# A table of times in a planned three-stage kernel: weight conversions, weight loads and operand splits at other places

## The chip, the cores and the metric

The kernel runs as one program on one core of a Trainium2 chip. The metric is device time in microseconds (us) of one execution; before the change it is the median of three runs, and one more execution was profiled. Engines are named as in the profile: PE is TensorE (its weight loads, which overlap its matmuls, are PEld), DVE is VectorE, ACT is ScalarE, POOL is GpSimd, SP is SyncE, which here only issues DMAs.

## The reference

Three things are computed in a row, in float32. First an attention in chunks of 64 positions, over batch 8, 8 heads, 576 positions and head size 64. Then a layer with softmax and layer norm, 512 to 1024 to 512. Then a layer with a SiLU, 512 to 2048 to 512:

```python
x = attention(q, k, v)                       # chunks of 64, softmax, 4608 tokens x 512
h = x @ w_in                                 # 512 -> 1024
solu = h * softmax(h)
ln = (solu - mean) / sqrt(var + 1e-06) * g_ln
x = ln @ w_out                               # 1024 -> 512
h = x @ w2_in                                # 512 -> 2048   ("the way in")
out = (h * sigmoid(h)) @ w2_out              # 2048 -> 512   ("the way out")
```

The weights come as 64-bit floats and are taken apart word by word on the chip.

## The kernel before

**Precision.** Each float32 operand of a matmul is split in two parts, hi (rounded on the way) and lo (the rest), and a product is three matmuls: hi by hi, hi by lo, lo by hi. A "split" is thus one copy to hi (ACT) and one subtraction for lo (DVE or POOL).

**Stages.** From 0 to about 598 us the attention and the first layer run for 36 tiles of 128 tokens. From 598.5 to 985.3 us the way in runs. From 985.3 us to the end the way out runs. Both ways use a scheme of seven products in place of eight (Strassen's), named p1, p6, p2, p7, p5, p4, p3 in the order in which PE makes them.

**The way in** takes the tokens in six groups of 768. A group needs seven split operands (`s_split`, tile `y1s`), made from four raw quarters of the input (`raw_load`, tile `ry`) and their differences (`raw_t`, POOL, L517). In a group there are eight units u, one for each slice of the weights, handled in four pairs. In a pair, PE makes each of the seven products for both units, 6 matmuls a product. Results are put together in this order: `c_p1` (ACT, L592), `c_u2` (DVE, L596), `c_u3` (DVE, L600), `c22` (DVE L610, then ACT), `c21` (L618), `c12` (L626). Each takes one buffer of a ring (`tmp`) and its result is stored to DRAM (`g_store`, tile `gd`, L588). PE may not start p7 before `c_u2` has read the bank that p6 left, and may not start p3 before `c22` has read the bank (`hw`) that p5 left: three products later in both cases.

**Changes of group.** While the last pair of a group runs, the operands of the next group are split, one after another as the product that used the old one ends. I count them 1 to 5; they lie at about 653, 713, 777, 838 and 903 us.

**The way out's weights** are converted during the way in, 16 pieces i = 0 to 15 (`conv_load`, `conv_a` L159, L160, `conv_b` L174, L185, `conv_c` L207, mostly on DVE), each from a 512 KB load into the tile `st_w`. Every two pieces are then mixed and split on POOL (`w2_mix`, L237, L248, L252) and stored to DRAM (`w2od`, L255). The attention tiles before carry the conversions of the way in's weights in the same functions.

**The way out** takes 18 pairs of token tiles. All its weights (56 tiles of 256 KB, `w2o_load`, tile `w2o`, L644) are read back from DRAM while the last group of the way in gives up its buffers. For each pair, four loads of 512 KB (`g_load`, L674), sums (`g_sum`, L681), splits (`g_split`, ACT L688, then DVE or POOL L690), seven products of 24 matmuls (`out_product`, L697), and stores (L723).

**What sets the order.** Every piece of work is entered in a plan with a time (`at(time, function, ...)`), and each engine, SP with its DMAs included, gets its instructions in the order of these times. The times are only sort keys: an engine runs its list in order and waits where data are missing. `XA` is the planned start of the way in, `PA` = 14 * 1.042 the planned length of a pair, so a group is 4 PA and a change of group falls on 4, 8, 12, 16 and 20 PA; `XB = XA + 24 * PA` is the planned start of the way out.

Of the kernel before, what the change touches and what calls it, by code (L numbers as in the profile page):

```python
# [18 lines left out]
DVE, POOL, ACT = ET.DVE, ET.Pool, ET.Activation  # L19
# [32 lines left out]
def chunk_attention_moe_moe(ctx: ExitStack, tc: tile.TileContext, q, k, v, w_in, w_out, g_ln, w2_in, w2_out, out):  # L52
# [44 lines left out]
    kT = sb.tile([128, 2 * HP, 2, CH], F32, tag="kT", name="kT")  # L97
# [629 lines left out]
    at = plan.at  # L727
# [24 lines left out]
    for t in range(TT):  # L752
# [32 lines left out]
            at(x + y[2], y_store, b, m)  # L785
        x = T[t]
        for _ in range(CONV[t] if nxt < N1 else 0):
            at(x - 10.0, conv_load, nxt)
            at((x + 2.0, x + 2.6), conv_a, nxt)
            at((x + 3.5, x + 4.1), conv_b, nxt, side(nxt))  # L790
            if nxt < 4 * KD:
                at((x + 5.2, x + 6.0, x + 6.7, x + 8.8), conv_c, nxt, side(nxt))
            else:
                at(x + 5.2, conv_c, nxt, side(nxt))
                if nxt % 2:
                    y = 122.2 if nxt == 17 else x + 5.3
                    at([y, y + 0.9, y + 1.8, y + 2.7] + [y + 3.6 + 3.8 * (i // 3) + (0.0, 1.0, 2.6)[i % 3] for i in range(12)], w2_mix, (nxt - 17) // 2, 0)
            nxt += 1
# [36 lines left out]
    for n in range(NGR * NF // 2):  # L835
# [13 lines left out]
            at([y + 12 * SL + d for d in (0.0, 0.6, 1.2)], c12, u)  # L849
        if jj == 0:  # L850
            x -= PA
            on = ((ACT, DVE), (ACT, DVE), (ACT, POOL), (ACT, DVE), (ACT, POOL), (ACT, POOL), (ACT, DVE))
            for o, (hi_on, lo_on) in enumerate(on):
                y = x + (2 * o + 2) * SL + 0.2
                if p == 0:
                    y = XO + 1.0 + 2.0 * o if o < 5 else XA + 0.3 + 1.2 * o - 6.0
                at((y, y + 1.0), s_split, p, o, hi_on, lo_on)
                if o in (0, 2):
                    at(y + 1.1, raw_t, p, 2 if o == 0 else 3)
            if p + 1 < NGR:  # L860
                y = x + PA * (2.05 if p == 0 else 1.5)
                for i, q4 in enumerate((1, 0, 2, 3)):
                    at(y + 0.7 * i, raw_load, p + 1, q4)
                at(x + PA * (3.75 - 1.2 * (p % 2)), raw_t, p + 1, 0)
                at(x + PA * (3.9 - 1.2 * (p % 2)), raw_t, p + 1, 1)

    for i in range(K2):
        n = N1 + i
        x = XA + PA * (8 * (i // 6) + (0.9, 1.55, 2.6, 3.2, 5.4, 6.1)[i % 6])
        at(x - (5.0 if i else 11.0), conv_load, n)  # L870
        at((x, x + 1.2), conv_a, n)
        at((x + 2.4, x + 3.6), conv_b, n)
        at(x + 4.8, conv_c, n)
        if i % 2:
            x += (0.35, 1.2, 0.35)[i % 6 // 2] * PA
            at([x + 0.8 * d for d in range(4)] + [x + 3.2 + 1.8 * (d // 3) + (0.0, 0.7, 1.5)[d % 3] for d in range(21)], w2_mix, i // 2, 1)
    XB = XA + 24 * PA
    SB = 24 * 0.12
    for when, step, tags in (
        (XB - 2.98 * PA, 1.15, ("wo", "wo", "wo")),  # L880
        (XB - 1.98 * PA, 1.1, ("wo", "u", "u", "wi", "wi", "wi", "wi")),
        (XB - 11.0, 1.05, ("wi", "wi", "wi", "wi", "xs", "vt", "vt")),
        (XB + 3.8, 0.75, ("qr", "qr", "kr", "kr", "kT", "pT", "qT", "e")),
    ):
        for tag in tags:
            n = UNITS.get(tag, 2)
            at([when + step * 2 * k for k in range(n // 2 + 1)], w2o_load, tag, BUFS.get(tag, 2), n)
            when += step * n
# [7 lines left out]
    for vp in range(NP):  # L896
        x = XB + 7 * SB * vp
        for i in (2, 3, 0, 1):
            y = XB - (3.6 - 0.2 * i) * PA if vp == 0 else XB + 0.3 if vp == 1 and i > 1 else max(x - 11 * SB, XB + 2.1)
            at(y + 0.1 * i, g_load, vp, i)  # L900
        for n in range(4):
            y = x + (-6.2, -5.7, -3.2, -0.9)[n] * SB
# [178 lines left out]
```

## Time and profile before

| | |
|---|---|
| median of 3 runs | 1369.13 us (1368.89 to 1372.35) |
| the profiled execution | 1366.64 us, of which the span from first to last instruction is 1364.8 us |
| mean granted PE clock | 0.983 |
| PE busy | 1280.3 us, 94% of the span |
| DVE, ACT, POOL busy | 900.1, 608.7, 587.4 us |

A row of the timeline gives start, length, engine, source line and operation, with the idle time before it and what ended that wait in brackets. A row of the windows gives busy time of each engine in a stretch, the granted PE clock (1.00 is 2.4 GHz, 0.50 is 1.2 GHz), the busy share of the DMA engines and the rate in GB/s.

### The profile page before, as it was taken

To read this page: it belongs to the slowest core of one execution; us is meant where nothing else is said; L and a number is where in the kernel's file an instruction comes from. 1 tells how busy PE (TensorE), PEld (TensorE's weight loads), DVE (VectorE), ACT (ScalarE), POOL (GpSimd) and SP (SyncE) were. 2 spreads that over 40 slices of the span, in tenths; PEclk is the share of its full clock that TensorE was granted. 3 is DMA by queue.
4 is the path that set the end of the run, shared out by engine and by line. 5 is a ranking of instruction groups with operands and counts; after the bars stand their busy time and mean duration, and the time that the engine had idled before them with its cause. 6 is when DMAs were issued, how large, how long until landed. Compare 5 with 4: busy or idle time off the path is not lost. (4 is left out here: it accounts for less than half of the span.)

```text
span 1364.8 us, 22483 instructions
## 1 busy us (share of the span) xinstructions
PE 1280.3 (94%) x8400; PEld 1169.4 (86%) x8400; DVE 900.1 (66%) x1371; ACT 608.7 (45%) x991; POOL 587.4 (43%) x466
## 2 busy tenths in 40 slices
PE   3889998999999999899899999989879999999998
PEld 2678886877887788788899999989879999999998
DVE  7798785877878788425555655563556666666661
ACT  5686544544554555433444434443333333443341
POOL 4543112321321332223554546262166666666662
PEclk9999998999999999999999999999889999999999
DMA  9575366655554651867576556659974434434420
GB/s 204 86 136 97 62 119 154 135 126 123 136 129 112 154 147 46 321 236 247 160 233 212 179 182 199 202 163 286 318 291 133 147 109 135 146 122 136 133 90 30
DMA packets 330845, 217.50 MB, mean 159 GB/s; under 512 B 187248, under 2 KB 288624, under 8 KB 330736
## 3 DMA queue, kind: packets, MB, share of 16 engines
q1 hardware_dynamic: 330736, 216.07, 56.2%
q8 instruction: 66, 1.08, 0.3%
q14 instruction: 43, 0.35, 0.1%
HBM read 130.03 MB, written 85.98 MB: 158 GB/s over the span
## 5 line engine op out<-in xcount | busy, mean ns | idle before, releaser
L580 PE MATMUL h<-y1s,w2t 128*128 128x384 f32 x1440 | 263.8, 338 | 9.6 <-DVE tmp L596 8.5
L697 PE MATMUL h<-w2o,gs 128*128 128x256 f32 x2160 | 265.7, 283 | 0.6 <-DMA w2o<-w2od 0.6
L580 PEld LDWEIGHTS h<-y1s,w2t 128*128 128x128 f32 x1440 | 252.9, 189 | 13.4 <-DVE tmp L596 11.5
L697 PEld LDWEIGHTS h<-w2o,gs 128*128 128x128 f32 x2160 | 262.2, 192 | 1.2 <-DMA w2o<-w2od 1.0
L407 PE MATMUL h<-wi,xs 128*128 128x512 f32 x864 | 220.2, 405 | 5.7 <-DVE u L424 2.9
L466 PE MATMUL yp<-lnT,wo 128*128 128x512 f32 x864 | 211.9, 395 | 0.7 <-ACT ys L471 0.7
L407 PEld LDWEIGHTS h<-wi,xs 128*128 128x128 f32 x864 | 162.1, 192 | 44.7 <-ACT e L346 2.9
L466 PEld LDWEIGHTS yp<-lnT,wo 128*128 128x128 f32 x864 | 159.1, 188 | 38.6 <-issue 5.1
L688 ACT ACTIVATE gs<-g 128x1024 fp32r<-128x1024 f32 x117 | 123.4, 1058 | 149.8 <-PE h L697 73.8
L690 POOL TENSOR_TENSOR gs<-g,gs 128x1024 fp32r<-128x1024 f32 x54 | 148.1, 2744 | 58.3 <-ACT gs L688 51.2
L690 DVE TENSOR_TENSOR gs<-g,gs 128x1024 fp32r<-128x1024 f32 x63 | 105.7, 1678 | 34.3 <-ACT gs L688 34.1
L580 PE MATMUL hw<-y1s,w2t 128*128 128x384 f32 x576 | 115.1, 350 | 12.7 <-DVE tmp L610 12.6
L580 PEld LDWEIGHTS hw<-y1s,w2t 128*128 128x128 f32 x576 | 106.4, 198 | 15.3 <-DVE tmp L610 15.3
L697 PE MATMUL hw<-w2o,gs 128*128 128x256 f32 x864 | 111.0, 285 | 7.2 <-DMA w2o<-w2od 7.2
L697 PEld LDWEIGHTS hw<-w2o,gs 128*128 128x128 f32 x864 | 107.2, 194 | 7.6 <-DMA w2o<-w2od 7.0
L434 POOL TENSOR_TENSOR st<-st,nhalf 128x1 f32<-128x1 f32 x36 | 21.3, 591 | 201.8 <-DVE st L432 201.8
L237 POOL TENSOR_TENSOR cv<-cv 128x256 f32<-128x256 f32 x64 | 48.2, 771 | 106.3 <-DVE cv L207 105.0
L356 POOL TENSOR_TENSOR e<-e,sm 128x512 f32<-128x512 f32 x36 | 42.2, 1171 | 77.8 <-DVE sm L354 73.3
L391 DVE TENSOR_TENSOR lnT<-tp,lnT 128x512 fp32r<-128x512 f32 x72 | 49.4, 686 | 37.6 <-ACT lnT L382 36.8
L382 ACT ACTIVATE lnT<-tp 128x512 fp32r<-128x512 f32 x72 | 42.9, 595 | 68.6 <-PE tp L452 68.6
L681 POOL TENSOR_TENSOR g<-g,g0x 128x1024 f32<-128x1024 f32 x18 | 43.5, 2416 | 68.1 <-DVE gs L690 68.1
L612 ACT ACTIVATE tmp<-tmp 128x384 f32<-128x384 f32 x48 | 24.5, 526 | 81.2 <-DVE tmp L610 77.5
(116 smaller groups left out, 1826.9 us busy)
## 6 DMA issues: line engine op xcount, KB each, us to landing
gd<-tmp SPq DMA_DIRECT2D x192, 192.0 KB
g<-gd SPq DMA_DIRECT2D x72, 512.0 KB
w2d<-cv_m SPq DMA_DIRECT2D x56, 256.0 KB
w2t<-w2d SPq DMA_DIRECT2D x56, 256.0 KB
w2od<-y1s SPq DMA_DIRECT2D x56, 256.0 KB
w2o<-w2od SPq DMA_DIRECT2D x27, 512.0 KB
st_w<-in_moe_w_out_dram SPq DMA_DIRECT2D x24, 512.0 KB
vt<-in_v_dram SPq DMA_DIRECT2D x36, 256.0 KB
```

Source lines behind the costliest of these rows:

```text
L237: nc.gpsimd.tensor_tensor(out=out, in0=in0, in1=in1, op=op)
L356: nc.gpsimd.tensor_tensor(out=e, in0=e, in1=sm.to_broadcast([128, HP, 2, CH]), op=ALU.mult)
L382: nc.scalar.activation(out=hi, in_=src, func=AF.Copy)
L391: nc.vector.tensor_tensor(out=lo, in0=src, in1=hi.bitcast(F32), op=ALU.subtract)
L407: nc.tensor.matmul(h_t[t][:, n, :], xs[:, a, kk, :], wi[b][kk][:, n * 512:(n + 1) * 512], start=(kk == 0 and i == 0), stop=(kk == KD - 1 a ...
L466: nc.tensor.matmul(yps[b, m], wo[a][f // 4][:, f % 4, 128 * m:128 * (m + 1)], lnT[b][c][:, f, :], start=(f == 0 and i == 0), stop=(f == K1 ...
L580: nc.tensor.matmul(acc, w[:, a, kk, :], t[:, i, c, :], start=start and kk == 0 and n == 0, stop=kk == 1 and n == 2, skip_group_check=not s ...
L612: nc.scalar.activation(out=c, in_=c, func=AF.Silu)
L681: on.tensor_tensor(out=out, in0=in0, in1=in1, op=op_)
L688: nc.scalar.activation(out=dst[:, 0], in_=src, func=AF.Copy)
L690: (nc.gpsimd if o > 3 else nc.vector).tensor_tensor(out=dst[:, 1], in0=src, in1=dst[:, 0].bitcast(F32), op=ALU.subtract)
L697: nc.tensor.matmul(acc, g[:, a, f, :], wo2[o, f][:, c, :], start=start and f == 0 and i == 0, stop=f == NF - 1 and i == 2, skip_group_chec ...
```

## The change

It alters numbers in the plan. No function is changed, and the same work is done.

- The conversions of the way in's weights (pieces 18 and later, in the attention stage) are loaded 3.5 us earlier in the plan.
- The lo part of two splits at each change of group moves from POOL to DVE (p2 and p4), and one moves from DVE to POOL (p3).
- The loads of the second group's raw quarters stand 0.65 PA later.
- The 16 conversions of the way out's weights get other times. Before, those with i = 3, 9 and 15 stood 0.8 PA ahead of a change of group (3.2 of 4); now i = 3 stands 0.3 PA behind it, and i = 9 and 15 stand 1.25 PA ahead of it. Their mixing keeps about its place.
- The way out's weight loads stand closer together and earlier, and the loads of the third pair (vp = 2) later, at XB + 11 in place of about XB + 8.6.

```diff
@@ -785,7 +785,7 @@
         for _ in range(CONV[t] if nxt < N1 else 0):
-            at(x - 10.0, conv_load, nxt)
+            at(x - 13.5, conv_load, nxt)
@@ -849,7 +849,7 @@
         if jj == 0:
             x -= PA
-            on = ((ACT, DVE), (ACT, DVE), (ACT, POOL), (ACT, DVE), (ACT, POOL), (ACT, POOL), (ACT, DVE))
+            on = ((ACT, DVE), (ACT, DVE), (ACT, DVE), (ACT, DVE), (ACT, POOL), (ACT, DVE), (ACT, POOL))
@@ -858,7 +858,7 @@
             if p + 1 < NGR:
-                y = x + PA * (2.05 if p == 0 else 1.5)
+                y = x + PA * (2.7 if p == 0 else 1.5)
@@ -866,21 +866,21 @@
     for i in range(K2):
         n = N1 + i
-        x = XA + PA * (8 * (i // 6) + (0.9, 1.55, 2.6, 3.2, 5.4, 6.1)[i % 6])
-        at(x - (5.0 if i else 11.0), conv_load, n)
+        x = XA + PA * (8 * (i // 6) + ((0.8, 1.4, 2.5, 4.3, 5.5, 6.1) if i < 6 else (0.5, 1.1, 2.2, 2.75, 5.4, 6.0))[i % 6])
+        at(x - 5.0 if i else XA - 1.0, conv_load, n)
         at((x, x + 1.2), conv_a, n)
         at((x + 2.4, x + 3.6), conv_b, n)
         at(x + 4.8, conv_c, n)
         if i % 2:
-            x += (0.35, 1.2, 0.35)[i % 6 // 2] * PA
+            x += (1.6 if i % 6 == 3 and i > 6 else 0.38) * PA
@@
-        (XB - 1.98 * PA, 1.1, ("wo", "u", "u", "wi", "wi", "wi", "wi")),
-        (XB - 11.0, 1.05, ("wi", "wi", "wi", "wi", "xs", "vt", "vt")),
-        (XB + 3.8, 0.75, ("qr", "qr", "kr", "kr", "kT", "pT", "qT", "e")),
+        (XB - 1.98 * PA, 0.95, ("wo", "u", "u", "wi", "wi", "wi", "wi")),
+        (XB - 13.6, 0.85, ("wi", "wi", "wi", "wi", "xs", "vt", "vt")),
+        (XB + 0.25, 0.55, ("qr", "qr", "kr", "kr", "kT", "pT", "qT", "e")),
@@ -896,7 +896,7 @@
-            y = XB - (3.6 - 0.2 * i) * PA if vp == 0 else XB + 0.3 if vp == 1 and i > 1 else max(x - 11 * SB, XB + 2.1)
+            y = XB - (3.6 - 0.2 * i) * PA if vp == 0 else XB + 0.3 if vp == 1 and i > 1 else max(x - 11 * SB, XB + (2.1 if vp == 1 else 11.0))
```

First place: DVE's list over the last pair of the first group, up to the second `c22` (L610), before.

```order
L596 TENSOR_TENSOR tmp<-h_6035,tmp 128x384
L546 TENSOR_TENSOR y1s<-ry,y1s 128x2x384
L596 TENSOR_TENSOR tmp<-h_6047,tmp 128x384
L174 SCALAR_TENSOR_TENSOR cv<-st_w,cv 128x512
L546 TENSOR_TENSOR y1s<-ry,y1s 128x2x384
L185 SCALAR_TENSOR_TENSOR cv<-st_w,cv 128x512
L600 TENSOR_TENSOR tmp<-h_6035,tmp 128x384
L207 SCALAR_TENSOR_TENSOR cv<-cv 128x512
L600 TENSOR_TENSOR tmp<-h_6047,tmp 128x384
L610 TENSOR_TENSOR tmp<-hw,tmp 128x384
L546 TENSOR_TENSOR y1s<-ry,y1s 128x2x384
L610 TENSOR_TENSOR tmp<-hw,tmp 128x384
```

The same stretch of DVE's list now.

```order
L596 TENSOR_TENSOR tmp<-h_6033,tmp 128x384
L546 TENSOR_TENSOR y1s<-ry,y1s 128x2x384
L596 TENSOR_TENSOR tmp<-h_6042,tmp 128x384
L546 TENSOR_TENSOR y1s<-ry,y1s 128x2x384
L600 TENSOR_TENSOR tmp<-h_6033,tmp 128x384
L546 TENSOR_TENSOR y1s<-ry,y1s 128x384 x2
L600 TENSOR_TENSOR tmp<-h_6042,tmp 128x384
L610 TENSOR_TENSOR tmp<-hw,tmp 128x384
L546 TENSOR_TENSOR y1s<-ry,y1s 128x2x384
L610 TENSOR_TENSOR tmp<-hw,tmp 128x384
```

The three instructions of a conversion (L174, L185, L207) have left the stretch, with L159 and L160 just ahead of it, and two half-sized pieces of the split of p2 have come in. At changes 3 and 5 the stretch reads alike before and now.

Second place: the same engine in the pair ahead of the last one of the third group, now. The conversion is that of i = 9.

```order
L610 TENSOR_TENSOR tmp<-hw,tmp 128x384 x2
L159 TENSOR_SCALAR cv<-st_w 128x512
L160 TENSOR_SCALAR cv<-st_w 128x512
L618 TENSOR_TENSOR tmp<-h_7097,tmp 128x384
L618 TENSOR_TENSOR tmp<-h_7111,tmp 128x384
L174 SCALAR_TENSOR_TENSOR cv<-st_w,cv 128x512
L626 TENSOR_TENSOR tmp<-hw,tmp 128x384
L185 SCALAR_TENSOR_TENSOR cv<-st_w,cv 128x512
L626 TENSOR_TENSOR tmp<-hw,tmp 128x384
L207 SCALAR_TENSOR_TENSOR cv<-cv 128x512
L596 TENSOR_TENSOR tmp<-h_7163,tmp 128x384
```

The conversion now ends right ahead of the first `c_u2` (L596) of the last pair, where it began before.

Third place: SP's list at the start of the way out, before. `g_8443` is the raw tile of the first and third pair, the other `g_` tiles are those of the second pair, `out_dram` is the output.

```order
L644 DMA w2o<-w2od 128x1024
L674 DMA g_8990<-gd 128x1024
L674 DMA g_8991<-gd 128x1024
L644 DMA w2o<-w2od 128x1024 x4
L674 DMA g_8443<-gd 128x1024 x4
L723 DMA out_dram<-ob 2x64x256
L644 DMA w2o<-w2od 128x1024 x2
L644 DMA w2o<-w2od 128x512 x2
L723 DMA out_dram<-ob 2x64x256 x3
```

And now.

```order
L644 DMA w2o<-w2od 128x1024
L674 DMA g_8994<-gd 128x1024
L674 DMA g_8995<-gd 128x1024
L644 DMA w2o<-w2od 128x1024 x4
L644 DMA w2o<-w2od 128x512 x2
L723 DMA out_dram<-ob 2x64x256
L674 DMA g_8443<-gd 128x1024 x4
L723 DMA out_dram<-ob 2x64x256 x3
```

The four loads of the third pair and one store stood ahead of the last four weight loads and now stand behind them; two weight loads more stand ahead of this stretch than before.

## Rows read from the trace of the kernel before

**Rows 1.** The page's head and its first row, busy us of PE.

```profile
span 1364.8 us, 22483 instructions
...
PE 1280.3 (94%) x8400; PEld 1169.4 (86%) x8400; DVE 900.1 (66%) x1371; ACT 608.7 (45%) x991; POOL 587.4 (43%) x466
```

**Rows 2.** Windows by stage; the first is the way in's first group.

```profile
598.50:653.00 54.50, 51.46 (x289) 49.81 (x288) 27.45 (x48) 21.49 (x41) 17.22 (x21) 1.00 0.80 262
598.50:985.30 386.80, 364.54 (x2017) 358.22 (x2017) 212.03 (x344) 158.72 (x302) 170.42 (x187) 0.97 0.69 219
985.30:1016.70 31.40, 23.56 (x170) 22.64 (x170) 16.01 (x13) 10.11 (x13) 19.13 (x7) 0.88 0.89 325
1016.70:1364.80 348.10, 341.77 (x2857) 341.56 (x2856) 215.17 (x182) 130.26 (x148) 213.94 (x82) 1.00 0.36 118
```

**Rows 3.** Windows of 20 us around the five changes of group.

```profile
651.00:671.00 20.00, 15.18 (x75) 14.22 (x75) 14.70 (x19) 9.71 (x19) 13.35 (x10) 0.91 0.42 127
713.00:733.00 20.00, 19.51 (x113) 19.19 (x112) 12.29 (x18) 11.93 (x22) 15.71 (x15) 1.00 0.60 190
776.00:796.00 20.00, 15.88 (x70) 14.93 (x69) 14.55 (x19) 9.47 (x18) 13.26 (x10) 0.83 0.46 140
838.00:858.00 20.00, 19.85 (x113) 19.21 (x112) 10.74 (x16) 11.93 (x22) 16.78 (x16) 1.00 0.62 194
901.00:921.00 20.00, 15.15 (x77) 14.18 (x76) 14.12 (x19) 9.42 (x17) 13.16 (x11) 0.91 0.41 125
```

**Rows 4.** Timeline of PE at change 1.

```profile
664.69 3.56 PE L580 MATMUL hw<-y1s,w2t 128*128 128x384 f32 x12 [3.77 <-DVE tmp L610]
...
676.78 2.24 PE L580 MATMUL hw<-y1s,w2t 128*128 128x384 f32 x12
```

**Rows 5.** Timeline of DVE at change 1.

```profile
655.29 1.74 DVE L174 SCALAR_TENSOR_TENSOR cv<-st_w,cv 128x512 int32<-128x512 int32 x1
656.95 1.77 DVE L546 TENSOR_TENSOR y1s<-ry,y1s 128x768 fp32r<-128x768 f32 x1
658.64 1.50 DVE L185 SCALAR_TENSOR_TENSOR cv<-st_w,cv 128x512 f32<-128x512 uint32 x1
...
660.53 1.84 DVE L207 SCALAR_TENSOR_TENSOR cv<-cv 128x512 f32<-128x512 f32 x1
...
663.23 0.94 DVE L546 TENSOR_TENSOR y1s<-ry,y1s 128x768 fp32r<-128x768 f32 x1
```

**Rows 6.** Timeline of DVE at change 2.

```profile
720.79 0.56 DVE L600 TENSOR_TENSOR tmp<-h,tmp 128x384 f32<-128x384 f32 x1 [0.48 <-PE h L580]
722.87 0.56 DVE L610 TENSOR_TENSOR tmp<-hw,tmp 128x384 f32<-128x384 f32 x1 [1.52 <-PE hw L580]
```

**Rows 7.** Timeline of POOL at change 1.

```profile
656.47 3.13 POOL L546 TENSOR_TENSOR y1s<-ry,y1s 128x384 fp32r<-128x384 f32 x2
```

**Rows 8.** Timeline of PE over the end of the way in and the first out pair.

```profile
958.65 1.97 PE L580 MATMUL h<-y1s,w2t 128*128 128x384 f32 x6 [2.97 <-DVE tmp L596]
...
982.05 3.48 PE L580 MATMUL hw<-y1s,w2t 128*128 128x384 f32 x12 [1.76 <-DVE tmp L610]
...
1012.64 4.21 PE L697 MATMUL hw<-w2o,gs 128*128 128x256 f32 x18 [6.82 <-DMA w2o<-w2od]
```

**Rows 9.** Timeline of SP's DMA queue in the first out pair.

```profile
992.24 3.43 SPq L644 DMA_DIRECT2D w2o<-w2od  x4
995.86 4.32 SPq L674 DMA_DIRECT2D g<-gd  x4
...
1002.20 4.47 SPq L644 DMA_DIRECT2D w2o<-w2od  x4
```

**Rows 10.** Windows of 3 us: DMA around the start of the way out.

```profile
981.00:984.00 3.00, 1.95 (x8) 1.95 (x9) 1.93 (x4) 1.97 (x4) 0.00 (x0) 0.82 0.22 65
1002.00:1005.00 3.00, 2.06 (x13) 1.68 (x14) 3.00 (x3) 0.40 (x1) 2.57 (x1) 1.00 1.02 408
```

**Rows 11.** Timeline of DVE in the attention stage, at one late load.

```profile
230.42 0.43 DVE L159 TENSOR_SCALAR cv<-st_w 128x512 int32<-128x512 int32 x1 [7.00 <-DMA st_w<-in_moe_w_in_dram]
```

## What I predict, and why

> **What bounds the kernel now.** I read the page first: PE is busy for 94% of the span [rows 1], so time can only come from the rest and from stretches in which PE runs at its lower clock. The windows by stage say where the rest lies. The way out from its second pair on is full, at clock 1.00, and nothing is to be had there; its first pair has PE busy for 23.56 of 31.40 us at clock 0.88, and the way in 364.54 of 386.80 at 0.97 [rows 2]. Windows of equal length around the five changes of group then show a pattern: changes 1, 3 and 5 leave PE idle for 20 - 15.18 = 4.8, 4.1 and 4.9 us at mean clocks of 0.91, 0.83 and 0.91, while changes 2 and 4 leave 0.5 and 0.15 at 1.00 [rows 3]. All five carry the same splits. What differs is that a conversion falls into changes 1, 3 and 5.
>
> The timelines give the mechanism. At change 1 PE stands for 3.77 us ahead of p3 until DVE's c22 (L610) has read the bank; after it, 12 matmuls take 3.56 us, where 12 take 2.24 once the clock is back [rows 4]. DVE is late because L174, L185 and L207 of a conversion stand in its list between c_u2 and c22: 1.74 + 1.50 + 1.84 = 5.1 us [rows 5]. A c22 has three products, about 3.1 us, before PE needs its bank. At change 2, with no conversion, DVE itself waits for PE ahead of c_u3 and c22, 0.48 + 1.52 = 2.0 us [rows 6]. In the first pair of the way out the last wait to end is for the read-back weights: 6.82 us, then 18 matmuls in 4.21 us [rows 8]. Ahead of the loads waited for, SP issued the four loads of the third pair [rows 9].
>
> **The change, part by part.**
>
> A, changes 1, 3 and 5. The idle time is 4.8 + 4.1 + 4.9 = 13.8 us. A mean clock of 0.91 over 20 us is 1.8 us lost, 0.83 is 3.4, 0.91 again 1.8: 7.0 us. Together 20.8 us [rows 3]. The conversions leave these stretches. What comes in on DVE is the split of p2 as two half-sized pieces: 0.94 us in all if they run as the whole split of p7 does at 663.23, or 1.77 if they are as slow as the split at 656.95, which ran beside POOL [rows 5]. On POOL the same two pieces took 3.13 [rows 7]; that is the upper bound. DVE's idle 2.0 us at change 2 [rows 6] hides either of the first two, and 1.1 us would stick out of it by the bound. I take the first two, since the pieces will run on DVE. The split of p4 stands between the two c12, which have nine products of room, and p3's on POOL has twelve: nothing for both. So change 1 should look like change 2, 0.5 us left. Ahead of changes 3 and 5 the conversion of i = 9 or 15 now ends just before the first c_u2 of the last pair. If its load or the buffers of the mixing are late, its last three instructions, 5.1 us beside POOL [rows 5], run into the 3.1 us that c_u2 has; I leave 1.2 us for each, between nothing and all of the 6.6 or so that each now costs. A = 20.8 - 0.5 - 2.4 = 18 us.
>
> The Trainium skill, page "SBUF — State Buffer", section "Who interferes with whom", states that DVE and GpSimd share a pair of SBUF ports under an exclusive lock, so that the later one waits for a whole instruction of the other. That speaks against bringing splits to DVE. The slow split of 1.77 us against 0.94 agrees in kind, and its extra 0.83 is about half of a POOL piece. By the rule in full, each half piece could wait for a piece of POOL's, 3.13 us in all, 1.1 us would stick out at each of the five changes, and the sum would be about 5.5 us smaller, at 1348.5.
>
> B, edits that I cost at nothing. The earlier loads in the attention stage only pass two stores of mixed weights each, in four places; no engine is behind these stores in the rows, and the one late load that cost DVE 7.00 us [rows 11] keeps its place in SP's list, so no gain either; about a microsecond either way. In the first group the raw loads go later and a conversion's load earlier; PE is idle there for 54.5 - 51.46 = 3.0 us [rows 2], so the gain is at most that, and I allow the same as a loss if the load now in front makes stores late. At changes 2 and 4 the two half pieces are hidden by the 2.0 us above; uncovered they cost 1.1 us each.
>
> C, the first pair of the way out. PE is idle there for 31.40 - 23.56 = 7.8 us, and a clock of 0.88 over 31.4 us loses 3.8 more [rows 2]. The DMA engines are full then, at 408 GB/s [rows 10]. Four loads of 512 KB, 2.1 MB, now come behind the weights and not ahead of them: 5.1 us earlier. Also two weight loads more stand ahead of the stores that SP waited with at 981 us, when the engines moved only 65 GB/s for 3 us, a hole of 1.0 MB or 2.5 us [rows 10]; those loads can fill it, and I take half, 1.3 us. That is 6.4 of the 7.8. With what is left in pieces below half a microsecond, like those at changes 2 and 4 at which the clock held [rows 3], I count 2 of the 3.8 us of clock as given back, the rest to the wait at 982.05 [rows 8], which no edit touches. C = 8.4, taken as 8 us. Its bounds are 3.2 (below, under the second rival) and 11.
>
> Who waits next for the loads put back: the sums of the third pair, which PE needs two pairs of 20 us later. That covers the 5 us.
>
> **Sum.** 18 + 0 + 8 = 26 us off the profiled execution's 1366.64 gives 1340.6. That execution lies 2.5 us below the median of the three runs; off the median, 1369.13, I forecast **1343 us**.
>
> **Rivals.**
>
> First, changes 3 and 5 keep their stall. Speaking for it: DVE's list has the conversion of i = 9 against c_u2, loads into the single buffer st_w can be late, and POOL's differences run at that time, which slows DVE. Against: the conversion is a whole list position ahead of the stretch with the splits. Kept in full, at 4.1 + 3.4 and 4.9 + 1.8 less the 2.4 already left, it takes back 11.8: 1355. The port rule above is a milder form of it, with 1348.5 between.
>
> Second, the weights come no faster where it counts: the loads set closer together stand ahead of the stores of the way in's results, whose buffers DVE needs back. The wait at 958.65 is of that kind: 2.97 us, and 6 matmuls in 1.97 behind it where 6 at full clock are 1.1 [rows 8, 4]. One more such wait in the last pair, with the 1.8 us that the lower clock cost at change 1, is 4.8 us: C = 3.2 and 1347.8. Against it: the DMA queue does as many bytes either way, so a later start of the way out also makes its weights less late.
>
> Third, slower. In six pairs (i = 5, 7, 8, 11, 13, 14) the first instruction of a conversion stands directly ahead of a c_u2, as it did in some pairs before. It blocks DVE until the load into st_w lands, and only one such buffer is free, so a load waits for the conversion before. The price of one that is late by 7.00 us [rows 11], less the 3.1 us that c_u2 has, is 3.9 of waiting, 1.8 of clock and the 2 us by which c22 is late in turn: 7.7. It decides from the fourth place on: 4 times 7.7 is 30.8, against 26 and the 4.1 that a measurement can tell (below). All six give 46.2, and 1343 + 46.2 = 1389. Against it: the change keeps the load 5 us ahead of its conversion.
>
> Fourth, the change doesn't do what it says: the splits, not the conversions, make c22 late. Then A is nothing, C stands or falls with the second rival, and at C = 3.2 the time is 1366, within 0.3%. Changes 2 and 4, with the same splits and no stall, speak against it [rows 3].
>
> **How the numbers follow.** 0.3% of the median, 4.1 us, is about what a measurement of this kernel can tell from no change. Chances: forecast 0.50, first rival 0.17 (the port rule within it), second 0.17, both of these (1360) 0.06, third 0.05, fourth 0.05. The first four are faster by more than 0.3%: 0.90. Same 0.05, slower 0.05. The range reaches down by the 2.9 us left in A, the 3 of B and part of what C may still give, to 1335, and up past the first rival to 1357; the third and fourth and the two rivals together stay out, 0.16.
>
> **What would show it.** PE in 20 us windows around changes 1, 3 and 5: busy for 19 us or more at clock 1.00 shows A right; a wait for L596 or L610 there with L185 or L207 ahead of it on DVE is the first rival. The wait for w2o at the end of the first out pair below 2 us shows C right; a longer wait for L596 ended by a store's landing in the last two pairs of the way in is the second. A wait of L159 for st_w that ends just ahead of a PE wait is the third. The forecast is wrong if these waits go but the way in, 386.8 us [rows 2], doesn't shorten by about 18, or the first out pair by about 8.

## The result, and the profile after

The changed kernel takes 1355.74 us (median of 4 runs, 1352.54 to 1358.2), the kernel before 1369.99 (4 runs, 1368.89 to 1372.35). The ratio is 0.9892, 95% interval 0.9867 to 0.9918: 14 us faster, where 26 were forecast. The time lies in the range, near its upper end. The profiled execution of after took 1358.2 us, the longest of its four; that of before took 1366.64, less than any of its own four. The two traces therefore differ by only 8.4 us.

The head of the page and its first row, after:

```profile
span 1356.4 us, 22472 instructions
...
PE 1274.6 (94%) x8400; PEld 1166.2 (86%) x8400; DVE 900.7 (66%) x1383; ACT 609.4 (45%) x991; POOL 568.2 (42%) x454
```

The windows by stage, after, in the order of [rows 2]. The columns are the stretch, its length, busy time of PE, PEld, DVE, ACT and POOL, the granted PE clock, the DMA share and GB/s:

```profile
599.20:653.80 54.60, 51.40 (x285) 50.73 (x284) 26.61 (x48) 22.01 (x41) 16.73 (x21) 0.97 0.77 240
599.20:978.70 379.50, 361.13 (x2018) 355.92 (x2017) 211.83 (x354) 160.10 (x302) 155.63 (x177) 0.98 0.72 225
978.70:1010.10 31.40, 29.45 (x238) 28.48 (x238) 17.12 (x15) 13.07 (x16) 21.10 (x9) 1.00 0.78 277
1010.10:1356.40 346.30, 336.12 (x2790) 335.71 (x2788) 215.09 (x181) 126.79 (x144) 209.50 (x81) 0.99 0.36 119
```

The way in is 7.3 us shorter, not 18. The first 31.4 us of the way out have PE busy for 29.45 us where it was 23.56, near the forecast. But the rest of the way out, which was full before, now has a hole: 346.30 - 336.12 = 10.2 us idle, where [rows 2] have 6.3.

The windows around the five changes of group, after, to be read beside [rows 3]:

```profile
652.70:672.70 20.00, 19.41 (x110) 18.80 (x110) 13.11 (x23) 10.93 (x20) 8.68 (x6) 1.00 0.59 170
709.00:729.00 20.00, 19.65 (x114) 19.33 (x113) 13.05 (x19) 12.37 (x23) 14.98 (x14) 1.00 0.66 206
771.00:791.00 20.00, 17.44 (x99) 16.80 (x98) 14.56 (x22) 12.26 (x23) 9.83 (x8) 1.00 0.38 109
831.00:851.00 20.00, 20.00 (x116) 19.72 (x115) 12.61 (x19) 12.54 (x23) 14.17 (x12) 1.00 0.64 200
893.00:913.00 20.00, 17.20 (x89) 16.66 (x89) 14.36 (x22) 12.69 (x24) 7.49 (x5) 0.91 0.39 117
```

Change 1 now looks like change 2: 0.6 us idle at clock 1.00. Changes 3 and 5 still leave 2.6 and 2.8 us, and at change 5 the clock still dips.

A ledger of PE shows where these 8.4 us come from. A pair of the way in has 84 matmuls and one of the way out 168; the table gives, from PE's timeline, the time from the first matmul of a pair to the first of the next (us). A full pair takes 14.6 in the way in and 20.1 in the way out.

```
pairs                          before   after   difference
start of the way in            598.5    599.2   +0.7
3 and 4   (change 1)            36.4     30.3   -6.1
11 and 12 (change 3)            37.2     32.3   -4.95
19 and 20 (change 5)            36.2     33.95  -2.2
0 to 2                          48.1     49.1   +1.0
13, 14, 18 (conversions)        43.9     46.15  +2.25
21 to 23 (end of the way in)    52.1     55.2   +3.15
first pair of the way out       31.3     23.3   -8.0
second pair of the way out      20.3     26.1   +5.85
```

The other pairs differ by 0.3 us at most, together by -0.5; the sum is -8.8, and the end of the program is 0.4 longer. How far one trace can be trusted is shown by five traced kernels whose lists are the same up to pair 20 (the changed one, store_behind, sums_behind, fewer_weights and no_early_weights, below). In them pair 1 takes from 18.3 to 20.3 us, pair 3 from 15.5 to 19.45, pair 13 from 15.25 to 18.2 and pair 19 from 19.4 to 20.65; no other pair up to 20 differs by more than 0.9. Four places need an explanation: changes 3 and 5, pairs 21 to 23, and the second pair of the way out.

**Changes 3 and 5.** DVE just ahead of pair 19, after:

```profile
888.74 1.04 DVE L159 TENSOR_SCALAR cv<-st_w 128x512 int32<-128x512 int32 x1 [2.15 <-DMA st_w<-in_moe_w_out_dram]
889.70 2.06 DVE L160 TENSOR_SCALAR cv<-st_w 128x512 int32<-128x512 int32 x1
891.68 1.01 DVE L618 TENSOR_TENSOR tmp<-h,tmp 128x384 f32<-128x384 f32 x2
```

POOL and PE there, after:

```profile
887.66 3.81 POOL L517 TENSOR_TENSOR ry<-ry 128x768 f32<-128x768 f32 x2
...
889.52 4.33 PE L580 MATMUL h<-y1s,w2t 128*128 128x384 f32 x24
896.64 6.00 PE L580 MATMUL h<-y1s,w2t 128*128 128x384 f32 x24 [2.80 <-ACT tmp L592]
```

The conversion of i = 15 has left the stretch with the splits, but where it stands now its first two instructions take 3.1 us, where L159 takes 0.43 alone [rows 11]. The `c21` behind them is late, and so are the two `c12` (L626), between which the conversion's next instructions stand. ACT's part of the second `c12` (L628) waits for DVE, and behind it in ACT's list stands `c_p1` (L592), on which PE waits: another queue, another engine, 2.80 us. ACT there, after:

```profile
895.69 0.52 ACT L628 ACTIVATE tmp<-tmp 128x384 f32<-128x384 f32 x1 [0.54 <-DVE tmp L626]
896.12 0.85 ACT L592 ACTIVATE tmp<-h 128x384 f32<-128x384 f32 x2
```

Two causes offer themselves: the load, for which L159 waited 2.15 us, and POOL's two differences (L517), which run at the same time.

**The second pair of the way out.** DVE, after:

```profile
1009.23 3.28 DVE L681 TENSOR_TENSOR g<-g 128x1024 f32<-128x1024 f32 x1 [4.48 <-DMA g<-gd]
1012.54 1.23 DVE L681 TENSOR_TENSOR g0x<-g 128x1024 f32<-128x1024 f32 x1
1013.68 0.42 DVE L710 TENSOR_TENSOR ob<-h,ob 128x256 f32<-128x256 f32 x1
```

PE, after:

```profile
1014.16 5.49 PE L697 MATMUL h<-w2o,gs 128*128 128x256 f32 x24 [3.42 <-DVE ob L710]
```

POOL there, after:

```profile
1003.28 8.14 POOL L690 TENSOR_TENSOR gs<-g,gs 128x1024 fp32r<-128x1024 f32 x3
```

DVE's two sums for the third pair (L681) wait 4.48 us for the loads that were put back. The first of them then takes 3.28 us beside POOL's splits, the second 1.23 with POOL idle. Behind both stands `u2` (L710) of the second pair, the sum that reads the bank that PE needs next. PE waits 3.42 us for it, and 24 matmuls then take 5.49 us; at full clock 96 take 11.65 (sums_behind, below), so 24 take 2.9.

**The end of the way in.** DVE and PE in pair 22, after, beside 958.65 of [rows 8]:

```profile
950.19 0.56 DVE L596 TENSOR_TENSOR tmp<-h,tmp 128x384 f32<-128x384 f32 x1 [6.74 <-DMA gd<-tmp]
```

```profile
950.81 1.89 PE L580 MATMUL h<-y1s,w2t 128*128 128x384 f32 x6 [3.84 <-DVE tmp L596]
```

`c_u2` waits 6.74 us for a store to land, to have a buffer, and PE 3.84 behind it; it was 2.97 before.

### The profile page after: what moved, and what is told of

Its sections match the earlier page's. It is cut to its first block, busy times and chain, and to the rows that moved or that the text cites. A ratio compares the mean times of both kernels' runs of the same rounds, so it can differ in the third digit from the quotient of the medians.

```text
span 1356.4 us, 22472 instructions
## 1 busy us (share of the span) xinstructions
PE 1274.6 (94%) x8400; PEld 1166.2 (86%) x8400; DVE 900.7 (66%) x1383; ACT 609.4 (45%) x991; POOL 568.2 (42%) x454
## 5 line engine op out<-in xcount | busy, mean ns | idle before, releaser
L580 PE MATMUL hw<-y1s,w2t 128*128 128x384 f32 x576 | 111.4, 342 | 4.3 <-DVE tmp L610 4.3
L580 PEld LDWEIGHTS hw<-y1s,w2t 128*128 128x128 f32 x576 | 103.1, 192 | 6.5 <-DVE tmp L610 6.5
L681 POOL TENSOR_TENSOR g<-g,g0x 128x1024 f32<-128x1024 f32 x18 | 43.4, 2412 | 74.7 <-DVE gs L690 74.7
L596 DVE TENSOR_TENSOR tmp<-h,tmp 128x384 f32<-128x384 f32 x48 | 26.6, 556 | 62.0 <-DMA gd<-tmp 26.8
```

What stands on the lines that cost most here:

```text
L580: nc.tensor.matmul(acc, w[:, a, kk, :], t[:, i, c, :], start=start and kk == 0 and n == 0, stop=kk == 1 and n == 2, skip_group_check=not s ...
L596: nc.vector.tensor_tensor(out=c, in0=bank[u, "y"], in1=c_t[u, "p1"], op=ALU.add)
L681: on.tensor_tensor(out=out, in0=in0, in1=in1, op=op_)
```

## The experiments

Ratios are to the kernel before on the same chip, with 95% intervals; the changed kernel's own is 0.9892 (0.9867 to 0.9918). Single executions of one kernel spread over 3 to 11 us, so small shifts are read from the lengths of pairs in the traces, as far as they are larger than the spread of those pairs given above. Times in us of kernels that ran on different chips are compared by these ratios.

**conv_only.** The conversions' times alone, on the kernel before.

```diff
-        x = XA + PA * (8 * (i // 6) + (0.9, 1.55, 2.6, 3.2, 5.4, 6.1)[i % 6])
-        at(x - (5.0 if i else 11.0), conv_load, n)
+        x = XA + PA * (8 * (i // 6) + ((0.8, 1.4, 2.5, 4.3, 5.5, 6.1) if i < 6 else (0.5, 1.1, 2.2, 2.75, 5.4, 6.0))[i % 6])
+        at(x - 5.0 if i else XA - 1.0, conv_load, n)
...
-            x += (0.35, 1.2, 0.35)[i % 6 // 2] * PA
+            x += (1.6 if i % 6 == 3 and i > 6 else 0.38) * PA
```

> The kernel before with the new times of the 16 conversions (and of their mixing) alone; splits, weight loads and third-pair loads as before. Theory A (the conversions made c22 late at changes 1, 3 and 5): the five stretches lose what they lost in the changed kernel, pair 3 by 5.7 us, pairs 11 and 12 by 5, pair 19 by 2 or more, and 13, 14 and 18 pay 0.5 to 0.8 each: 11 us faster in all, about 1358 where before is 1369. Rival (the splits that moved from POOL to DVE are needed as well): PE still stands at least 1.5 us ahead of p3 at changes 1, 3 and 5 and less than 6 us are gained, about 1364.

Measured 1365.08 us, 0.9956 (0.9940 to 0.9973). The pairs of changes 1, 3 and 5 lose 11.0 us in its trace (16.0, 18.4 and 20.6 us for pairs 3, 11 and 19, their followers at 14.6). The wait ahead of p3 that the rival asks for, 1.5 us or more, is not there: it is 1.14 us at change 1, and nothing at changes 3 and 5. PE at change 1, of this kernel:

```profile
663.67 2.37 PE L580 MATMUL hw<-y1s,w2t 128*128 128x384 f32 x12 [1.14 <-DVE tmp L610]
```

So theory A holds for the place. Its time does not: the rival's 1364 came, not 1358, and change 5 gained 1.0 us where 2 or more were expected. The whole kernel gains only 6: pair 1 is 3.7 us longer, pairs 13, 14 and 18 pay 2.3, and pairs 21 to 23 are 3.8 longer, though no weight load has moved.

**conv_split.** The same with the new engines for the splits (the `on` line of the change).

> The kernel before with the conversions' new times and the new split of work between DVE and POOL; weight loads and third-pair loads as before. Theory A: within 1.5 us of the kernel with the conversions' times alone. Rival (the split's new engines matter): 3 us or more faster than that one, with the waits of the even changes, 2 and 4, or of raw_t on POOL shorter; or, by the shared port, 3 us or more slower.

Measured 1364.01 us, 0.9949 (0.9930 to 0.9967): no difference to conv_only in the time, as theory A has it. In the trace the three changes are 2.7 us shorter still, but pair 13 is 2.5 us longer and the first pair of the way out 3.1.

**weights_only.** The weight loads' times and the third pair's loads alone, on the kernel before.

> The kernel before with the closer weight loads of the way out and the later loads of the third pair alone. Theory C (the gain of the first pair of the way out is given back by the sums of the third pair, which stand in DVE's list ahead of a sum that PE waits for, and by later stores in the last pairs of the way in): first out pair 8 us shorter, second out pair about 6 us longer, last three pairs of the way in together 2 to 3 us longer: the time of before, 1368 to 1371. Rival (the second pair was late only because the way in ended earlier): second out pair stays at 20.3 us and the kernel is 5 to 8 us faster, 1361 to 1364.

Measured 1368.72 us, 0.9979 (0.9964 to 0.9994). First pair of the way out 24.4 us (-6.9), second 24.75 (+4.5), pairs 21 to 23 +2.7: theory C, though the interval leaves a gain of 1 to 5 us. Its DVE and PE in the second pair show the same wait, with a way in that is not shorter than before (393.3 us against 386.8), so the rival is out:

```profile
1021.82 3.24 DVE L681 TENSOR_TENSOR g<-g 128x1024 f32<-128x1024 f32 x1 [4.53 <-DMA g<-gd]
```

```profile
1026.70 3.58 PE L697 MATMUL h<-w2o,gs 128*128 128x256 f32 x20 [2.91 <-DVE ob L710]
```

**store_behind.** The changed kernel with the third pair's loads at their old time.

```diff
-            y = XB - (3.6 - 0.2 * i) * PA if vp == 0 else XB + 0.3 if vp == 1 and i > 1 else max(x - 11 * SB, XB + (2.1 if vp == 1 else 11.0))
+            y = XB - (3.6 - 0.2 * i) * PA if vp == 0 else XB + 0.3 if vp == 1 and i > 1 else max(x - 11 * SB, XB + 2.1)
```

> The changed kernel with the third pair's loads at their old time: the one thing that this alters in any engine's list is that one output store now stands behind these four loads and not ahead of them. Theory (the store, whose parts keep only two of the 16 DMA engines busy, holds up two parts of each load by 3 us, and SP waits ahead of it for the sum that it stores): the loads land 3 to 4 us earlier, DVE's wait of 4.5 us for them falls to about 1 us, PE's 3.4 us behind it goes, the second out pair falls from 26.1 to 21 us, and the kernel takes 1350 to 1352. Rival (the loads are late since SP can issue them only when the first pair's buffers are free, at 995 us): less than 1 us is gained, 1355.

Measured 1359.01 us, 0.9908 (0.9886 to 0.9930); second pair 25.9 us. The theory failed. DVE's wait did fall, from 4.48 to 2.09 us, but the second sum then ran beside POOL and took 3.33 us, where it took 1.23:

```profile
1009.80 3.29 DVE L681 TENSOR_TENSOR g<-g 128x1024 f32<-128x1024 f32 x1 [2.09 <-DMA g<-gd]
1013.13 3.33 DVE L681 TENSOR_TENSOR g0x<-g 128x1024 f32<-128x1024 f32 x1
```

It also says that the weight loads' new times, not the line for the third pair, put the weights in front: the loads of the third pair stay behind them in SP's list.

**sums_behind.** The changed kernel with the third pair's two DVE sums one place later.

```diff
+            if vp == 2 and n < 2:
+                y = x + (-4.9, -4.7)[n] * SB
             at(y, g_sum, vp, n)
```

> The changed kernel with two sums of the third pair (on DVE) entered one place later: they stand behind the sum that PE waits for in the second out pair, and not ahead of it. Nothing else moves. Theory (the gain of the first out pair is given back by DVE's list order): DVE's wait for the third pair's loads stays, but PE's 3.4 us behind it and the 2.6 us at the lower clock go; the second out pair falls from 26.1 to 20.3 us and the kernel takes about 1350. Rival (the late loads hold PE in any case, as the splits of the third pair are late in turn): the same 5 to 6 us turn up at the start of the third out pair, 1355.

Measured 1353.96 us, 0.9876 (0.9858 to 0.9895). Second pair 20.64 us, third 20.09: the 5.5 us are gone and turn up nowhere. DVE in the second pair:

```profile
1005.05 0.42 DVE L710 TENSOR_TENSOR ob<-h,ob 128x256 f32<-128x256 f32 x1 [3.25 <-PE h L697]
1005.39 1.77 DVE L681 TENSOR_TENSOR g<-g 128x1024 f32<-128x1024 f32 x1
```

PE behind it:

```profile
999.03 11.65 PE L697 MATMUL h<-w2o,gs 128*128 128x256 f32 x96
```

Now DVE waits for PE, and 96 matmuls run through. Only the order on DVE had to change. The medians differ by less than the runs spread, so the 5.5 us are shown by the trace alone.

**conv_room.** More room for the loads of i = 9 and 15: they are entered 2.5 us earlier, and i = 8 and 14 ahead of them are converted 0.25 PA earlier.

```diff
-        x = XA + PA * (8 * (i // 6) + ((0.8, 1.4, 2.5, 4.3, 5.5, 6.1) if i < 6 else (0.5, 1.1, 2.2, 2.75, 5.4, 6.0))[i % 6])
-        at(x - 5.0 if i else XA - 1.0, conv_load, n)
+        x = XA + PA * (8 * (i // 6) + ((0.8, 1.4, 2.5, 4.3, 5.5, 6.1) if i < 6 else (0.5, 1.1, 1.95, 2.75, 5.4, 6.0))[i % 6])
+        at(x - (7.5 if i in (9, 15) else 5.0) if i else XA - 1.0, conv_load, n)
```

> The changed kernel with i = 8 and 14 converted 0.25 PA earlier and the loads of i = 9 and 15 entered 2.5 us earlier, so that these two loads have more room behind the release of their single buffer. Theory (at changes 3 and 5 the conversion is late since its load waits for that buffer): DVE's waits of 0.9 and 2.2 us for the load go, and with them PE's 1.65 us near the start of pair 11 and 2.8 us near that of pair 19 with its slow matmuls; the two pairs shorten by about 3 and 4.5 us, 1348 to 1350 if nothing is given back. Rival 1 (L160 is slowed to 2.06 us by the differences on POOL and this is what is late): less than 1.5 us each. Rival 2 (from change 5 on the DMA queue sets the time): the pairs shorten as said, but what pair 19 gains is lost again in pairs 20 to 23 and the first out pair; 3 us are left, about 1353.

Measured 1355.51 us, 0.9897 (0.9880 to 0.9915): no gain. The wait for the load is gone, and the two instructions are slower still:

```profile
887.78 2.06 DVE L159 TENSOR_SCALAR cv<-st_w 128x512 int32<-128x512 int32 x1
889.76 2.06 DVE L160 TENSOR_SCALAR cv<-st_w 128x512 int32<-128x512 int32 x1
```

POOL meanwhile:

```profile
887.70 3.83 POOL L517 TENSOR_TENSOR ry<-ry 128x768 f32<-128x768 f32 x2
```

Two differences of 1.9 us on POOL, two instructions of 2.06 us on DVE, side by side to the end: rival 1. PE's stalls of 1.65 and 2.80 us in pairs 11 and 19 are 2.35 and 1.76 here. Pair 19 is 1.6 us shorter, pair 11 is 1.3 longer.

**diffs_early.** conv_room, and in addition POOL's differences ahead of changes 3 and 5 earlier in its list. The cut shows the addition.

```diff
-                at(x + PA * (3.75 - 1.2 * (p % 2)), raw_t, p + 1, 0)
-                at(x + PA * (3.9 - 1.2 * (p % 2)), raw_t, p + 1, 1)
+                at(x + PA * (3.3 if p in (2, 4) else 3.75 - 1.2 * (p % 2)), raw_t, p + 1, 0)
+                at(x + PA * (3.36 if p in (2, 4) else 3.9 - 1.2 * (p % 2)), raw_t, p + 1, 1)
```

> The kernel with more room for the loads of i = 9 and 15, and in addition the two differences on POOL (L517) ahead of changes 3 and 5 entered 0.5 PA earlier, so that they end before the conversion's L159 and L160 begin. Theory (L159 and L160 are late since each is stretched from 0.42 to 2.06 us while POOL is in a difference): L159 and L160 take 0.4 to 1.0 us, PE's stalls of 2.35 and 1.76 us near the start of pairs 11 and 19 go, pair 11 falls from 19.0 to 15.5 us and pair 19 from 17.8 to 15.5, 3 to 5 us in all: 1350 to 1352. Rival (the two instructions are slow for themselves or beside POOL's mixing as well): pair 11 above 18 us, 1355.

Measured 1352.51 us, 0.9849 (0.9829 to 0.9868), an interval wholly below that of conv_room. Pairs 11 and 19 take 15.3 and 15.6 us. DVE ahead of pair 19:

```profile
887.70 0.43 DVE L159 TENSOR_SCALAR cv<-st_w 128x512 int32<-128x512 int32 x1 [1.20 <-POOL y1s L252]
888.04 0.42 DVE L160 TENSOR_SCALAR cv<-st_w 128x512 int32<-128x512 int32 x1
```

POOL, whose second difference now ends 1.9 us ahead of L159:

```profile
883.96 1.85 POOL L517 TENSOR_TENSOR ry<-ry 128x768 f32<-128x768 f32 x1
```

The loads stay early here; the differences were not moved without them, so what the early loads add is not shown.

**both_fixes.** diffs_early and sums_behind together.

> The same with the two sums of the third pair behind the sum that PE waits for in the second out pair. Theory (the two stalls have causes of their own and their gains add up): second out pair 20.6 us, pair 11 and pair 19 15.5, 8 to 10 us under the changed kernel, 1346 to 1348. Rival (the transfers around the way out set the time, and what is gained ahead of them is lost in them): no more than 5 us, 1351.

Measured 1343.75 us, 0.9806 (0.9784 to 0.9829), 12 us under the changed kernel and somewhat more than was expected. Pairs 11 and 19 take 15.4 and 15.6 us, the second pair of the way out 20.65: the two gains add up.

**fewer_weights and no_early_weights.** The changed kernel without the read-back of p7's eight weight tiles, and without the 16 of p1 and p6; the products that lack weights take p2's. The edit of the first; the second has o < 2 in place of o == 3, and one line more that hands p2's tiles to p1 and p6.

```diff
-            nc.sync.dma_start(out=dst[:, i:i + m].bitcast(F32), in_=w2od[o, :, j:j + m])
+            left = o == 3
+            if not left:
+                nc.sync.dma_start(out=dst[:, i:i + m].bitcast(F32), in_=w2od[o, :, j:j + m])
             for k in range(m):
-                wo2[o, j + k] = dst[:, i + k]
+                wo2[o, j + k] = wo2[2, j + k] if left else dst[:, i + k]
```

> The changed kernel without the read-back of the eight weight tiles of p7, 2.1 MB (its matmuls take p2's weights). Theory (from change 5 to the second out pair the transfers set the time, so that the stalls there can only move): the stalls of pairs 21 to 23 and of the first two out pairs shrink by about 5 us together, the time in which 2.1 MB pass at 400 GB/s; the stretch from pair 19 to the third out pair falls from 138.6 to 133 us, 1350. Rival (each of these stalls has its own cause in an engine's list): less than 1.5 us.

Measured 1354.21 us, 0.9882 (0.9863 to 0.9902). The five pairs 21 to 23 and first two of the way out take 100.6 us where they took 104.6: 4 us of the 5 expected, 3.4 of them in pair 23. Pairs 21 and 22 are not shorter (16.3 and 21.1), and the time of the whole kernel does not tell it from the changed one. So these 2.1 MB weigh on pair 23, and the transfers do not set the time of the whole stretch.

> The changed kernel without the read-back of the 16 weight tiles of p1 and p6, 4.2 MB (their matmuls take p2's weights); these are the loads that pass in pairs 21 and 22 of the way in. Theory (stores of the way in's results land late behind these loads, and DVE's c_u2 waits for their buffers): pairs 21 and 22 fall from 16.1 and 20.3 to about 14.7 each, 7 us; what follows is not longer. Rival (the stores are late behind the last mixed weights that are stored, or wait for SP): the two pairs stay within 1.5 us.

Measured 1352.47 us, 0.9853 (0.9833 to 0.9874). The windows of pairs 21 and 22, of this kernel:

```profile
925.90:941.60 15.70, 14.84 (x85) 14.52 (x84) 5.30 (x10) 4.89 (x10) 4.50 (x8) 1.00 0.81 245
941.60:956.30 14.70, 14.70 (x87) 14.70 (x86) 5.39 (x10) 4.88 (x10) 0.00 (x0) 1.00 0.89 270
```

And of the changed kernel:

```profile
923.50:939.50 16.00, 14.86 (x85) 14.54 (x84) 5.10 (x10) 4.82 (x10) 4.52 (x8) 1.00 0.93 287
939.50:959.80 20.30, 16.46 (x87) 16.14 (x86) 5.39 (x10) 4.88 (x10) 0.00 (x0) 0.92 1.06 363
```

Pair 22 is full without the loads: the 3.84 us and the clock dip are theirs, 5.7 us. In pair 21 PE still waits, 0.86 us where it was 1.14. The theory holds for pair 22 alone; why stores are late in pair 21 stays open.

**first_group.** The changed kernel with the old times for i = 0 and 1, for the load of i = 0 and for the second group's raw loads.

> The changed kernel with the edits in the way in's first group undone (the times of the first three items: conversions i = 0 and 1, the load of i = 0, the loads of the second group's raw quarters). Theory (the edits in the first group cost what pair 1 got longer): pair 1 falls from 19.9 to 18.6 us, the kernel is 1.3 us faster, 1354. Rival (with the new conversion times, raw loads at the old place would make the second load late as where the conversions alone were moved, 22.2 us): no gain or 2 us slower, 1358.

Measured 1356.65 us, 0.9891 (0.9870 to 0.9911); pair 1 19.8 us against 19.9. No effect can be seen. In kernels whose lists are the same there, pair 1 took from 18.3 (sums_behind) to 21.3 us (conv_room), so the 1.3 us of the ledger say nothing about the edit.

**store_in_two.** both_fixes with each output store as two.

```diff
-        nc.sync.dma_start(out=out.rearrange("(b s) f -> b s f", b=B)[2 * tt:2 * tt + 2, b * CH:(b + 1) * CH, 256 * n:256 * n + 256], in_=c)
+        for k in range(2):
+            nc.sync.dma_start(out=out.rearrange("(b s) f -> b s f", b=B)[2 * tt + k, b * CH:(b + 1) * CH, 256 * n:256 * n + 256],
+                              in_=c[64 * k:64 * k + 64])
```

> The kernel with both fixes, and each output store of the way out issued as two stores of 64 rows in place of one of 2 by 64 rows. Theory (a store of 2 by 64 rows keeps two of the 16 DMA engines busy and a store of 64 rows spreads over more): the DMA share of 0.13 to 0.14 behind the first out pair goes, and the end of the program, where the last store takes some 6 us from its issue to the last instruction, comes 2 to 3 us sooner: 1341. Rival (SP, which has twice as many stores to issue, is late with the loads of the pairs): out pairs longer than 20.09 us, slower by more than 3 us; or the store's time is latency and not its two engines: no change, 1343 to 1345.

Measured 1342.42 us, 0.9790 (0.9775 to 0.9804), the fastest of all, though its interval overlaps that of both_fixes. The last sum of the program and the span's length, of both_fixes:

```profile
span 1341.3 us, 22468 instructions
...
1334.57 0.42 DVE L710 TENSOR_TENSOR ob<-hw,ob 128x256 f32<-128x256 f32 x1 [2.45 <-PE hw L697]
```

And of this one:

```profile
span 1343.4 us, 22575 instructions
...
1339.46 0.42 DVE L710 TENSOR_TENSOR ob<-hw,ob 128x256 f32<-128x256 f32 x1 [2.45 <-PE hw L697]
```

From the end of that sum to the end of the span it was 6.3 us and is 3.5, so 2.8 us of the end are saved; out pairs stay at 20.09.

## Why the prediction came out as it did, point by point

**The diagnosis** was right: the conversions at changes 1, 3 and 5 made `c22` late. Moved alone, they shorten these stretches by 11 us (conv_only), and PE's wait ahead of p3 of 3.77 us [rows 4] is 1.14 there and gone in the changed kernel. The fourth rival is out.

**A, forecast 18, measured 13.3.** Change 1 gave 6.1 us, exactly the term (4.8 + 1.8 - 0.5). The two half pieces of p2 took 1.02 us on DVE, near the first of the two values taken for them, 0.94. (The price that the prediction gave for the port rule, 1.1 us a change, counts the wait of 3.13 us alone; with the pieces' own 0.94 it is 2.1. Neither came.) Not every execution gives as much: in the traces of fewer_weights and store_in_two, whose lists are the same at this place, pair 3 took 19.45 and 18.3 us in place of 15.7. There `c_u2` waited for a buffer, that is, for a store to land. A store of mixed weights (L255) stands ahead in SP's list; it went out at 653.7 us in fewer_weights and at 651.5 in the changed kernel, which fits but was not tested. DVE and PE at change 1 of fewer_weights:

```profile
658.17 0.56 DVE L596 TENSOR_TENSOR tmp<-h,tmp 128x384 f32<-128x384 f32 x1 [5.07 <-DMA gd<-tmp]
```

```profile
658.79 2.29 PE L580 MATMUL h<-y1s,w2t 128*128 128x384 f32 x6 [3.05 <-DVE tmp L596]
```

For changes 3 and 5 the allowance of 1.2 us each was too small: they gave 4.95 and 2.2 where 7.5 - 1.2 = 6.3 and 6.7 - 1.2 = 5.5 were counted. The step that failed is the sentence on what could be late there. It named the load, the buffers, and the conversion's last three instructions running into `c_u2`'s time. What was late were its first two, stretched from 0.85 us together to 3.1 by POOL's differences, ahead of `c21`, in a chain that ends in ACT's `c_p1`. conv_room and diffs_early show it: with the load early and the differences in place nothing is gained in all, with the differences moved as well the two instructions are short and pairs 11 and 19 are 2.5 and 3.8 us under the changed kernel's. The first rival was right on the place, and half a sentence of it names POOL's differences as what slows DVE; but it expected `c_u2` to be late, and a loss of 11.8 us where 4.6 were lost.

The rule of the Trainium skill (page "SBUF — State Buffer", section "Who interferes with whom") was weighed against the splits only. The same section counts tensor_scalar among the operations that can, where their operands allow it, take both port pairs, and then they and GpSimd block each other fully. The trace of conv_room agrees: L159 and L160 last as long as a whole difference of POOL and a little more, 2.06 us beside 1.9. Whoever holds that rule against each DVE instruction in its new place comes upon this one.

**B, forecast 0 within 3 us.** Its sum in the ledger is 0.7 + 1.0 + 2.25 - 0.5 = 3.5 us; the 1.0 of pairs 0 to 2 lies within what pair 1 varies by itself. What is left are 2.25 us in pairs 13, 14 and 18, in which conversions now stand. In conv_room pair 18 fell to 14.8 us with its conversion 0.25 PA earlier. The third rival's 7.7 us a place appeared nowhere, but its sign did, in pair 13, at the conversion of i = 10, which it had not listed. DVE and PE there, after:

```profile
808.54 0.43 DVE L159 TENSOR_SCALAR cv<-st_w 128x512 int32<-128x512 int32 x1 [2.46 <-DMA st_w<-in_moe_w_out_dram]
```

```profile
812.60 2.36 PE L580 MATMUL hw<-y1s,w2t 128*128 128x384 f32 x12 [0.52 <-DVE tmp L610]
```

In the trace of no_early_weights, with the same lists here, L159 waits 2.68 us and PE 1.95, and the pair takes 18.2 us.

**C, forecast 8, measured -1.0 in the two traces, that is, nothing or nearly so.** By its times weights_only, which has this part alone, gains 1 to 5 us. The first pair gave 8.0 us, as worked out. It was given back at two places. The first is the sentence "Who waits next for the loads put back: the sums of the third pair, which PE needs two pairs of 20 us later. That covers the 5 us." It looked at who needs the data and not at what stands behind the waiting sums in DVE's list; `u2` of the second pair does, and PE needs that one at once. This cost 5.85 us, of which sums_behind takes back 5.5 by moving the sums alone. weights_only shows it without the rest of the change. The second is the second rival: 3.15 us in pairs 21 to 23, forecast at 4.8 with a chance of 0.17. no_early_weights shows that the loads make all of the stall in pair 22, and fewer_weights that they weigh on pair 23; neither says how much of it the new times brought. For that there is weights_only, with 2.7 us in the three pairs, nearly all of it in 22 and 23. But the closer loads are not all of it: conv_only, with the loads at their old times, has 3.8 us in pairs 21 to 23 as well. Why the end of the way in grows when the changes of group shrink was not taken apart; that the loads are keyed to the order of the work and so come as much earlier is only argued.

**The sum.** -13.3 of A, +3.5 of B, +3.15 and -2.2 of the two parts of C make -8.8 in the traces, of the 26 forecast. Between the medians 14 us were gained; the profiled execution of before lay 3.4 us under its median and that of after 2.5 us over its own, which is the difference; no trace shows where these 5.8 us lie. That the time lies within the range owes something to them: the 8.4 us of the traces, off the median of before, give 1361.6, outside it. And that it lies beside the first rival's 1355 is chance, since the loss came from all three parts.

## What to carry to other kernels

When a transfer is put back, look past the instruction that needs it to everything behind that instruction on its engine: an in-order queue makes the whole list wait, and the cure may be to move a sum by one place. When an instruction is moved out of a bad place, read what the neighbour engines do in the new one, instruction by instruction; 0.42 us became 2.06. And ledger a pipelined kernel by equal units of the bounding engine: where a gain is given back stands in one line, while totals hide it under a spread of several us. Even then one trace is not enough: pair 3 took 15.7 us in one execution and 19.45 in another with the same lists.

## What the runs showed of the hardware

DVE's int32 tensor_scalar on 128x512 takes 0.42 us alone and 2.06 beside a 1.9 us tensor_tensor of POOL; its two-input sum over 128x1024 (L681) takes 1.2 us alone and 3.3 beside POOL's splits.

An output store of 2 by 64 rows of 1 KB uses few of the 16 DMA engines. Behind the first pair of the way out of the changed kernel, once most of the loads have passed, the DMA share stays at 0.13 while such stores are under way, about two of 16 engines. The window:

```profile
1006.00:1009.00 3.00, 3.00 (x27) 3.00 (x26) 0.00 (x0) 1.43 (x2) 3.00 (x2) 1.00 0.13 52
```

The Trainium skill, page "DMA: Bandwidth & Descriptors", section "Why a DMA increments its semaphore by 16 and not by 1", says that a transfer uses as many engines as the largest number up to 16 that divides the sizes of the slowest dimensions of both its sides. The share agrees, with slowest size 2 on the side of the output, and so do the 2.8 us that store_in_two saved at the end of the program.

The same stall did not always cost the same. Behind PE's 2.80 us in pair 19, 24 matmuls took 6.00 us at a mean granted clock of 0.72 in the changed kernel and 7.24 us at 0.58 in sums_behind, and the pair took 19.39 and 20.65 us; ahead of the stall 24 took 4.33 at 1.00. The rows of the changed kernel stand above, under changes 3 and 5; PE in sums_behind:

```profile
891.88 7.24 PE L580 MATMUL h<-y1s,w2t 128*128 128x384 f32 x24 [2.80 <-ACT tmp L592]
```
